# Two edits to a retention-attention and mixture-of-experts kernel: one weight chunk's low part made by GpSimd instead of an accumulating DMA, and a table of powers spread by TensorE instead of loaded whole

## The chip, the cores and the metric

The kernel runs on one core of one Trainium2 chip. The metric is the device time of one execution, in microseconds (us). Engine names are those of the profile: PE is TensorE, ACT is ScalarE, DVE is VectorE, POOL is GpSimd, SP is SyncE, which here only issues DMAs and waits.

## What is computed

The first half is retention attention over 8 batches, 8 heads, 576 positions and head size 64. The second half is a mixture of 8 experts whose input is the attention's output, 4608 tokens of 512 numbers. Each expert takes 576 tokens.

```python
scores = scale * np.matmul(q, k.transpose(0, 1, 3, 2))
gamma = 1.0 - 2.0 ** (-5.0 - np.arange(H, dtype=np.float32))
Dmat = np.where(rel >= 0, gamma[:, None, None] ** rel[None, :, :], 0.0)
attn_out = np.matmul(scores * Dmat, v)
...
logits = x @ w_gate
# tokens go to experts in falling order of their logits, at most N // E = 576 to each
for e in range(E):
    mask = assigned == e
    out[mask] = np.maximum(x[mask] @ w1[e], 0.0) @ w2[e]
```

## The kernel before, in words

**Attention.** `attention` (L498) works through 16 units; a unit u is four batches' worth of one pair of heads, with its own loads of q, k, v and a second layout of k (`qin`, `kin`, `vin`, `nin`). The loads sit in three buffers each, and the load of unit u + 2 is issued when unit u begins. The decay is split in two factors: v is scaled by negative powers (`vscale`, L545, on ACT), and the output by positive powers when it leaves PSUM (`evict`, L621, on DVE, which multiplies by `ex`). `ex` is a [128, 4 x 576] table, the last part of the constants `cst`: for the pair of heads hp, partition p holds 0.125 times the powers 0 to 575 of one head's gamma, one head in partitions 0 to 63 and the other in 64 to 127. Its four pieces of 128 x 576 are loaded by `consts` (L521), two of them among the first loads, the other two when units 1 and 2 begin. `fetch` (L526) issues the first loads on SP in the order of a string; one of them, `q0`, goes out on ACT's queue.

Each half of a unit is a run of small fp32 matmuls: `A` (L557, tile `pA`) makes scores, which DVE masks into `am`; `ST` (L582, tile `pS`) makes the running state, which ACT copies to `S`; `across` and `within` (L594, L604, tile `pX`) make the output. The engines run their instructions in the order in which they are written here (the scheduler is switched off), so an instruction that waits holds up all that stand behind it on its engine. Small pieces of other work are hung on places of the loop with `at(g, ...)`, where g counts nine places to a unit, and `fills` runs them at the end of a half unit.

**Routing and experts.** After the attention, DVE and PE search for the tokens of the first expert (`search_first`, `members`, `listing`), GpSimd gathers their rows with five indirect DMAs (`gather`, L914), and the expert's two matmul layers run. The search for the next expert is threaded through the layers: its counting matmuls (`r`, L332) stand at fixed places among the layer's matmuls, and DVE's small operations (`cs` to `G`) between two counts make the operand of the next.

Weights come in chunks of 128 x 1024: each expert has four of w1 and four of w2, numbered 0 to 7 here. `conv` (L893) takes the next chunk out of `raw` and splits it in a high part `hi` and the rest `lo`, so that three fast matmuls stand in for one in full fp32:

```python
A.activation(hi, raw, AF.Copy)
if fast:
    V.tensor_tensor(lo, raw, hi.bitcast(F32), op=ALU.subtract)
else:
    A.activation(lo, raw, AF.Copy, scale=-1.0)
    nc.gpsimd.dma_start(lo, raw, accum_op=ALU.add)
```

So DVE makes the low part of chunk 0 of the first expert (`conv(True)` in `run`); for all others ACT writes a negated rounded copy and an accumulating DMA, issued by GpSimd, adds `raw` to it. `raw` has four buffers: `dma_pump` (L880) issues the load of a chunk into a buffer once both readers of the chunk that lay there are done.

`l1` (L941) runs the first layer in blocks (f, s): f is one of eight groups of 128 hidden columns, s a part of the tokens (256 or 320 of them); chunk f // 2 holds the weights. A block is 12 matmuls in groups of three, `wh` with `xh`, `wh` with `xl`, `wl` with `xh`; each block ends with ACT's `hb` (L967) and DVE's `hb` (L970). For the first expert the blocks run (0,0), (1,0), (0,1), (1,1), (2,0), (2,1) and on. `conv` is called after the blocks that this line picks (i counts blocks):

```python
if s and f in (1, 2, 4, 6) or e == 0 and i in (0, 2, 4):
    conv()
```

Of the kernel before, what the change touches and what calls it, by code (L numbers as in the profile page):

```python
# [10 lines left out]
F32 = mybir.dt.float32  # L11
# [3 lines left out]
ALU = mybir.AluOpType  # L15
AF = mybir.ActivationFunctionType
AX = mybir.AxisListType

B, H, S, D = 8, 8, 576, 64
NP, HP, NB = 4, 4, 9  # L20
# [5 lines left out]
def consts_np():  # L26
    h = np.arange(H); g = (1.0 - 2.0 ** (-5.0 - h)).astype(np.float64)
    p = np.arange(128)
    at = np.where(np.arange(NB) < 8, 128 * (np.arange(NB) // 2), 512)[None] + np.where(np.arange(NB) < 8, p[:, None], p[:, None] % 64)
    vs = g.reshape(HP, 1, 2)[None] ** -at[:, None, :, None].astype(np.float64)  # L30
    m1 = p[:, None] <= p[None, :]
    m2 = p[:, None] % 64 <= np.arange(64)[None, :]
    ex = 0.125 * g.reshape(HP, 2)[:, p // 64].T[:, :, None] ** np.arange(S)
    f = lambda a: np.ascontiguousarray(a, dtype=np.float32).reshape(128, -1)
    return np.concatenate([f(vs), f(m1), f(m2), f(ex)], axis=1)

# [41 lines left out]
class Route:  # L78
# [9 lines left out]
    def fetch(s, nc, fc_d):  # L88
        s.nc = nc
        s.fc = s.pool.tile([128, fc_d.shape[1]], F32, name="rc_f")  # L90
        nc.sync.dma_start(s.fc, fc_d)
# [405 lines left out]

def attention(tc, nc, P, qk, vk, cst_d, wg_d, rf, xd, Lg):  # L498
    cst = P['c'].tile([128, CST + HP*S], F32, name="cst", tag="xg")
    vs = cst[:, 0:HP*18].rearrange("p (h q) -> p h q", h=HP)  # L500
    m1, m2 = cst[:, CST-192:CST-64], cst[:, CST-64:CST]
    ex = cst[:, CST:].rearrange("p (h q) -> p h q", h=HP)
    wg = P['a'].tile([128, HP, 32], F32, name="wg")
# [16 lines left out]

    def consts(hp):  # L521
        part(CST + S*hp, CST + S*hp + S)
    load(0, "kqvn", (512,))
    load(1, "kqvn", (512,))

    def fetch(order):  # L526
        for x in order.split():
            if x == "c":
                part(0, CST)
            elif x[0] == "h":  # L530
                consts(int(x[1]))
            else:
                (nc.scalar if x == "q0" else nc.sync).dma_start(*pieces[x[0].isupper(), x[0].lower()].pop(0))
    fetch("k0 q0 c v0 n0 k1 q1 h0 v1 n1 K0 Q0 h1 V0 N0 K1 Q1 V1 N1")
    R = Route(P['c'], P['a'], P['ps'], Lg, P['ident'])
# [17 lines left out]
    def A(u, hf):  # L553

        if u == 16: return
        if hf == 0 and 2 <= u + 1 < 16:
            if u < 3:  # L557
                consts(u + 1)
            if u == 2:
                R.fetch(nc, rf)  # L560
                nc.sync.dma_start(wg[:, :, 0:8], wg_d.rearrange("(hp p) e -> p hp e", p=128))
# [191 lines left out]
    A(0, 0)  # L753
    ST(0, 0)
    nc.gpsimd.memset(wg, 0.0)

# [96 lines left out]
def moe(tc, nc, P, R, xd, w1_d, w2_d, out, mix):  # L853
# [38 lines left out]

    def conv(fast=False):  # L893

# [9 lines left out]
        if fast:  # L904
            V.tensor_tensor(lo, raw, hi.bitcast(F32), op=ALU.subtract)
        else:
            A.activation(lo, raw, AF.Copy, scale=-1.0)
            nc.gpsimd.dma_start(lo, raw, accum_op=ALU.add)  # L908
# [32 lines left out]
    def l1(e, tr):  # L941
# [5 lines left out]
        for i, (f, s) in enumerate(order):  # L947
# [24 lines left out]
            mix.vec(340 + 140*s)  # L972
            if s and f in (1, 2, 4, 6) or e == 0 and i in (0, 2, 4):
                conv()
# [61 lines left out]
    def run():  # L1036
# [3 lines left out]
        gather(0)  # L1040
        conv(True)
        mix.step()
        warm(25)
        mix.adv(3500)
# [14 lines left out]

def build(tc, nc, qk, vk, cst, wg, rf, w1, w2, out):  # L1060
    with ExitStack() as top:
        P = {}
# [31 lines left out]
        with ExitStack() as ctx:  # L1094
            Q = dict(P)
            for name, bufs in (("a", 1), ("ld", 2), ("w", 2), ("xt", 2)):
                Q[name] = ctx.enter_context(tc.tile_pool(name="a_" + name, bufs=bufs))
            R, rows = attention(tc, nc, Q, qk, vk, cst, wg, rf, xd, Lg)

# [35 lines left out]
```

## Time and profile before

| | |
|---|---|
| three runs | 650.55, 650.63, 651.21 us; median 650.63 us |
| the profiled execution | 651.56 us |
| its span, first to last instruction | 649.8 us |
| PE busy in the span | 610.9 us (94%) |
| DVE, ACT, POOL busy | 406.5, 288.8, 140.9 us |
| mean granted TensorE clock | 0.986 |
| moved by DMA | 134.20 MB |

The page gives the busy time of each engine and the chain of work that ended last. The timeline rows read: start, duration, engine, line, operation, output <- input, shape, count; in square brackets the idle time of the engine before the row and who ended it. A row with a count over 1 merges instructions that followed each other. Rows marked SPq are DMA issues of the SP queue.

### The profile page before, as it was taken

How to read it: one execution, taken by the hardware profiler on the slowest of the kernel's cores; microseconds unless marked ns; L12 is line 12 of the kernel's file. 1: busy time of each engine (PE TensorE's matmuls, PEld its weight loads, DVE VectorE, ACT ScalarE, POOL GpSimd, SP SyncE). 2: the span in 40 equal slices, each digit the busy share in tenths (PEclk: the TensorE clock that was granted, in tenths of full speed). 3: DMA queues.
4: the chain of work that ended last, by engine and by line, in shares of the span. 5: the costliest groups of instructions: out<-in, count | busy, mean ns of one | idle time of the engine just before them, and what ended most of it. 6: DMA issues, size and time to landing. Idle time of an engine off the chain costs nothing.

```text
span 649.8 us, 14770 instructions
## 1 busy us (share of the span) xinstructions
PE 610.9 (94%) x5756; PEld 519.3 (80%) x5756; DVE 406.5 (63%) x1504; ACT 288.8 (44%) x584; POOL 140.9 (22%) x189
## 2 busy tenths in 40 slices
PE   8899898978969998999999999988999999999995
PEld 5687777756569878977987898788779889989984
DVE  3567979778747887987996897777783302301300
ACT  4455555523265236552563356144615724643500
POOL 0000000000311072162153142241314234131111
PEclk9999999989979999999999999998999999999998
DMA  9998999743497469889599199747966995893521
GB/s 333 400 391 281 348 350 351 266 98 131 155 215 176 140 173 246 212 193 263 110 245 261 59 223 227 208 106 172 201 188 146 227 264 141 174 269 117 98 66 40
DMA packets 51704, 134.20 MB, mean 207 GB/s; under 512 B 5810, under 2 KB 19762, under 8 KB 51634
## 3 DMA queue, kind: packets, MB, share of 16 engines
q0 software_dynamic: 14960, 51.91, 36.7%
q1 hardware_dynamic: 36530, 81.08, 36.0%
q8 instruction: 45, 0.74, 0.5%
q10 hardware_dynamic: 144, 0.26, 0.1%
q14 instruction: 25, 0.20, 0.1%
HBM read 81.33 MB, written 18.87 MB: 154 GB/s over the span
## 4 chain that ended last, share of the span: by engine, by line
PE 68%; DVE 15%; DMA 6%; issue 6%; POOL 2%; ACT 2%; SPq 0%; POOLq 0%; DVEq 0%; ACTq 0%
PE ph L963 25%; PE py L1002 24%; PE pA L566 4%; PE pX L610 3%; DMA qin<-in_qk 2%; PE pS L589 2%; PE pX L601 2%; PE r L332 2%; PE pt L934 2%; DMA w1l<-raw 1%; PE pT L643 1%; DVE am L568 1%; DVE xT L630 1%; POOL xg L919 1%; DMA cst<-in_cst 1%
## 5 line engine op out<-in xcount | busy, mean ns | idle before, releaser
L1002 PE MATMUL py<-w2h,hb 128*128 128x512 f32 x576 | 188.2, 399 | 0.0
L963 PE MATMUL ph<-xh,w1h 128*128 128x320 f32 (+1 forms) x512 | 153.7, 304 | 2.7 <-ACT xh L936 1.5
L963 PE MATMUL ph<-xh,w1l 128*128 128x320 f32 (+1 forms) x512 | 151.3, 299 | 4.6 <-DMA w1l<-raw 4.2
L963 PE MATMUL ph<-xl,w1h 128*128 128x320 f32 (+1 forms) x512 | 151.0, 299 | 0.2 <-issue 0.2
L1002 PE MATMUL py<-w2l,hb 128*128 128x512 f32 (+1 forms) x320 | 125.1, 391 | 0.0
L1002 PEld LDWEIGHTS py<-w2h,hb 128*128 128x128 f32 x576 | 104.0, 188 | 20.6
L963 PEld LDWEIGHTS ph<-xh,w1l 128*128 128x128 f32 x512 | 97.7, 192 | 5.4 <-DMA w1l<-raw 4.4
L967 ACT ACTIVATE hb<-ph 128x256 fp32r<-128x256 f32 (+1 forms) x128 | 51.7, 410 | 112.5 <-PE ph L963 103.9
L963 PEld LDWEIGHTS ph<-xh,w1h 128*128 128x128 f32 x512 | 97.8, 192 | 4.7 <-ACT xh L936 1.9
L963 PEld LDWEIGHTS ph<-xl,w1h 128*128 128x128 f32 x512 | 97.9, 192 | 0.7 <-DVE cs L336 0.3
L970 DVE SCALAR_TENSOR_TENSOR hb<-ph,hb 128x256 fp32r<-128x256 f32 (+1 forms) x192 | 59.0, 352 | 60.2 <-ACT hb L967 56.6
L919 POOL DMA_INDIRECT xg<-xd,idx x40 | 40.8, 1020 | 202.1 <-DMA raw<-in_w 168.8
L1002 PEld LDWEIGHTS py<-w2l,hb 128*128 128x128 f32 (+1 forms) x320 | 56.7, 177 | 12.7
L979 POOL DMA_INDIRECT out_y<-yt,idx x40 | 40.9, 1022 | 118.4 <-ACT yt L1019 76.4
L1019 ACT ACTIVATE yt<-py 128x512 f32<-128x512 f32 x32 | 19.2, 598 | 105.3 <-PE py L1002 79.8
L908 POOL DMA_DIRECT2D w2l<-raw x32 | 28.8, 900 | 126.5 <-ACT hb L967 117.8
L548 ACT ACTIVATE vin<-vin,cst 128x128 f32<-128x128 f32 (+1 forms) x160 | 48.2, 379 | 6.8 <-DMA vin<-in_vk 6.8
L568 DVE TENSOR_TENSOR am<-pA,cst 128x1024 f32<-128x1024 f32 x32 | 39.1, 1221 | 18.0 <-PE pA L566 17.7
L1022 DVE TENSOR_TENSOR yt<-yt,py 64x512 f32<-64x512 f32 x8 | 5.4, 679 | 69.5 <-ACT yt L1021 69.3
L566 PEld LDWEIGHTS pA<-qin,kin 64*128 64x128 f32 x512 | 32.1, 191 | 16.1 <-DVE am L568 7.8
L566 PE MATMUL pA<-qin,kin 64*128 64x128 f32 x512 | 38.3, 289 | 6.9 <-DVE am L568 5.0
L591 ACT ACTIVATE S<-pS 128x128 f32<-128x128 f32 x64 | 17.6, 276 | 51.1 <-PE pS L589 51.1
(177 smaller groups left out, 877.4 us busy)
## 6 DMA issues: line engine op xcount, KB each, us to landing
raw<-in_w SPq DMA_DIRECT2D x64, 512.0 KB, 5.5
w2l<-raw POOLq DMA_DIRECT2D x32, 512.0 KB
w1l<-raw POOLq DMA_DIRECT2D x31, 512.0 KB
kin<-in_qk SPq DMA_DIRECT2D x14, 576.0 KB, 7.2
qin<-in_qk SPq DMA_DIRECT2D x14, 576.0 KB
vin<-in_vk SPq DMA_DIRECT2D x14, 576.0 KB, 7.2
nin<-in_vk SPq DMA_DIRECT2D x14, 512.0 KB, 10.5
xd<-xr SPq DMA_DIRECT2D x36, 192.0 KB, 4.0
```

The lines of the kernel that those rows point to most:

```text
L548: nc.scalar.activation(x, x, AF.Copy, scale=vs[:, u % HP, 4*c+h:4*c+h+1])
L566: nc.tensor.matmul(pa[:, r, j], LD[u, 'k'][half(r), s], LD[u, 'q'][half(r), s], start=True, stop=True, skip_group_check=True)
L568: nc.vector.tensor_tensor(AM[u, hf], pa, m1[:, None, None, :].to_broadcast([128, 2, 4, 128]), op=ALU.mult)
L610: nc.tensor.matmul(PX[u, hf][half(h), b, 128*c:128*c+128], v[:, a:a+64], AM[u, hf][:, h ^ b, j], start=False, stop=False, skip_group_check ...
L908: nc.gpsimd.dma_start(lo, raw, accum_op=ALU.add)
L919: nc.gpsimd.indirect_dma_start(out=xg[:n, j, :], out_offset=None, in_=xd[:, :], in_offset=bass.IndirectOffsetOnAxis(ap=found[e][:n, j:j+1] ...
L963: T.matmul(ps, w, x, start=(k == 0), stop=(k == 11))
L967: A.activation(hb[:, f, c], ps, AF.Relu)
L970: V.scalar_tensor_tensor(hb[:, f, to+a:to+b], ps[:, a:b], 0.0, hb[:, f, 256*s+a:256*s+b].bitcast(F32), op0=ALU.max, op1=ALU.subtract)
L979: st = nc.gpsimd.indirect_dma_start(out=out[:, :], out_offset=bass.IndirectOffsetOnAxis(ap=found[e][:n, t:t+1], axis=0), in_=y[:n], in_off ...
L1002: T.matmul(ps[:m], a, w, start=(k == 0), stop=(k == last), skip_group_check=True)
L1019: A.activation(y, ps, AF.Copy)
```

## The change

Two edits that don't touch each other.

First, the table `ex` is no longer part of the constants in memory. For each pair of heads a [2, 704] array `er` is loaded: two rows, one for each head, with a 0/1 pattern of 128 columns that says which partitions belong to that head, and the head's 576 powers. `spread(hp)` makes the 128 x 576 table of the pair with two fp32 matmuls (contraction over 2 rows, 128 output rows, 288 columns each) and two ACT copies from PSUM. The four loads of `er` stand behind the constants on SP; `spread(0)` runs before the loop, the others at the places 4, 13 and 22.

Second, the split of chunk 1 of the first expert: its `conv` moves from behind block (0,0) to behind the gathers, and its low part is a subtraction on GpSimd.

```diff
-def attention(tc, nc, P, qk, vk, cst_d, wg_d, rf, xd, Lg):
-    cst = P['c'].tile([128, CST + HP*S], F32, name="cst", tag="xg")
+def attention(tc, nc, P, qk, vk, cst_d, er_d, wg_d, rf, xd, Lg):
+    cst = P['a'].tile([128, CST], F32, name="cst")
+    er = [P['c'].tile([2, 128 + S], F32, name="er", tag="raw", bufs=4) for _ in range(HP)]
...
-    ex = cst[:, CST:].rearrange("p (h q) -> p h q", h=HP)
+    ex = P['c'].tile([128, HP, S], F32, name="ex", tag="xg")
...
-    def consts(hp):
-        part(CST + S*hp, CST + S*hp + S)
+    def spread(hp):
+
+        for a in (0, S//2):
+            pe = P['ps'].tile([128, S//2], F32, name="pe", tag="y", bufs=2)
+            nc.tensor.matmul(pe, er[hp][:, :128], er[hp][:, 128+a:128+a+S//2], start=True, stop=True)
+            nc.scalar.activation(ex[:, hp, a:a+S//2], pe, AF.Copy)
...
-            elif x[0] == "h":
-                consts(int(x[1]))
+            elif x == "e":
+                for i in range(HP):
+                    nc.sync.dma_start(er[i], er_d[:, i*(128+S):(i+1)*(128+S)])
...
-    fetch("k0 q0 c v0 n0 k1 q1 h0 v1 n1 K0 Q0 h1 V0 N0 K1 Q1 V1 N1")
+    fetch("k0 q0 c e v0 n0 k1 q1 v1 n1 K0 Q0 V0 N0 K1 Q1 V1 N1")
...
-            if u < 3:
-                consts(u + 1)
...
     ST(0, 0)
+    spread(0)
+    for hp in range(1, HP):
+        at(9*hp - 5, spread, hp)
...
-    def conv(fast=False):
+    def conv(fast=None):
...
         if fast:
-            V.tensor_tensor(lo, raw, hi.bitcast(F32), op=ALU.subtract)
+            fast.tensor_tensor(lo, raw, hi.bitcast(F32), op=ALU.subtract)
...
-            if s and f in (1, 2, 4, 6) or e == 0 and i in (0, 2, 4):
+            if s and f in (1, 2, 4, 6) or e == 0 and i in (2, 4):
                 conv()
...
         gather(0)
-        conv(True)
+        conv(V)
         mix.step()
+        conv(nc.gpsimd)
         warm(25)
```

The order of the first DMAs on SP. Before (`cst` 128x264 is the masks and small constants, `cst` 128x576 a piece of the table):

```order
L533 DMA kin<-in_qk 128x512
L519 DMA cst<-in_cst 128x264
L533 DMA vin<-in_vk 128x512
L533 DMA nin<-in_vk 128x512
L533 DMA kin<-in_qk 128x640
L533 DMA qin<-in_qk 128x640
L519 DMA cst<-in_cst 128x576
L533 DMA vin<-in_vk 128x640
L533 DMA nin<-in_vk 128x512
L533 DMA kin<-in_qk 128x512
L533 DMA qin<-in_qk 128x512
L519 DMA cst<-in_cst 128x576
```

Now:

```order
L544 DMA kin<-in_qk 128x512
L525 DMA cst<-in_cst 128x264
L542 DMA er<-in_er 2x704 x4
L544 DMA vin<-in_vk 128x512
L544 DMA nin<-in_vk 128x512
L544 DMA kin<-in_qk 128x640
L544 DMA qin<-in_qk 128x640
L544 DMA vin<-in_vk 128x640
L544 DMA nin<-in_vk 128x512
L544 DMA kin<-in_qk 128x512
L544 DMA qin<-in_qk 128x512
```

Four small issues have come in ahead of the first `vin`, and the pieces of the table, which stood between the other loads, are gone.

The first matmuls of the attention on PE. Before:

```order
L566 MATMUL pA<-qin,kin 128x128 x8
L589 MATMUL pS<-vin,nin 64x64 x4
L566 MATMUL pA<-qin,kin 128x128 x8
L577 MATMUL pAt<-qin,kin 64x64 x4
L601 MATMUL pX<-qin,S 64x128 x4
```

Now:

```order
L575 MATMUL pA<-qin,kin 128x128 x8
L598 MATMUL pS<-vin,nin 64x64 x4
L531 MATMUL pe<-er 128x288 x2
L575 MATMUL pA<-qin,kin 128x128 x8
L586 MATMUL pAt<-qin,kin 64x64 x4
L610 MATMUL pX<-qin,S 64x128 x4
```

The first spread stands between the first state matmuls and the second group of scores. The other three stand each ahead of a group of scores as well: of the second half of units 1, 2 and 3.

ACT around the first layer of the first expert. Before (`xh` is the high part of the gathered tokens; the first `w1h` is chunk 0, the second chunk 1):

```order
L903 ACTIVATE w1h<-raw 128x1024
L936 ACTIVATE xh<-pt 128x4x128 x2
L967 ACTIVATE hb<-ph 128x256
L903 ACTIVATE w1h<-raw 128x1024
L907 ACTIVATE w1l<-raw 128x1024
L936 ACTIVATE xh<-pt 128x4x128 x2
L936 ACTIVATE xh<-pt 128x4x64
L967 ACTIVATE hb<-ph 128x256
L967 ACTIVATE hb<-ph 128x320
L903 ACTIVATE w1h<-raw 128x1024
L907 ACTIVATE w1l<-raw 128x1024
L967 ACTIVATE hb<-ph 128x320
```

Now:

```order
L915 ACTIVATE w1h<-raw 128x1024 x2
L948 ACTIVATE xh<-pt 128x4x128 x2
L979 ACTIVATE hb<-ph 128x256
L948 ACTIVATE xh<-pt 128x4x128 x2
L948 ACTIVATE xh<-pt 128x4x64
L979 ACTIVATE hb<-ph 128x256
L979 ACTIVATE hb<-ph 128x320
L915 ACTIVATE w1h<-raw 128x1024
L919 ACTIVATE w1l<-raw 128x1024
L979 ACTIVATE hb<-ph 128x320
```

The high part of chunk 1 has moved ahead of all token work and its negated copy is gone; chunk 2 and those after it keep their places. On POOL the first accumulating DMA behind the five gathers has become a `TENSOR_TENSOR` on the same tiles.

## Rows read from the trace of the kernel before

**Rows 1.** The page: the busy share of PE in 40 equal slices of 16.2 us, and the granted TensorE clock in the same slices, in tenths.

```profile
PE   8899898978969998999999999988999999999995
...
PEclk9999999989979999999999999998999999999998
```

**Rows 2.** The longest waits: engine and line, what ended the wait, us in total, times, longest.

```profile
PE ph L963 <- DMA w1l<-raw: 4.2, 1, 4.2
ACT vin L548 <- DMA vin<-in_vk: 6.8, 4, 2.4
```

**Rows 3.** Timeline of the first expert's first layer, ACT: chunk 0's high part, the first `xh`, then block (0,0), chunk 1 and on.

```profile
169.14 1.06 ACT L903 ACTIVATE w1h<-raw 128x1024 fp32r<-128x1024 f32 x1 [1.90 <-DMA raw<-in_w]
174.14 0.60 ACT L936 ACTIVATE xh<-pt 128x512 fp32r<-128x512 f32 x1 [3.94 <-PE pt L934]
...
178.46 1.05 ACT L903 ACTIVATE w1h<-raw 128x1024 fp32r<-128x1024 f32 x1
179.41 1.05 ACT L907 ACTIVATE w1l<-raw 128x1024 fp32r<-128x1024 f32 x1
180.36 1.35 ACT L936 ACTIVATE xh<-pt 128x512 fp32r<-128x512 f32 x3
...
183.82 0.44 ACT L967 ACTIVATE hb<-ph 128x320 fp32r<-128x320 f32 x1 [1.84 <-PE ph L963]
...
198.14 0.37 ACT L967 ACTIVATE hb<-ph 128x256 fp32r<-128x256 f32 x1
```

**Rows 4.** Timeline, PE, the same stretch: the first row is block (0,1), the next the third matmul of block (2,0), the last the third count.

```profile
181.76 0.85 PE L963 MATMUL ph<-xh,w1h 128*128 128x320 f32 x4 [0.80 <-ACT xh L936]
...
189.96 0.58 PE L963 MATMUL ph<-xh,w1l 128*128 128x256 f32 x1 [4.18 <-DMA w1l<-raw]
...
201.96 0.39 PE L332 MATMUL r<-oh,G 128*128 128x32 bf16 x9 [0.23 <-DVE G L163]
```

**Rows 5.** Timeline, POOL: the fifth gather, then the accumulating DMAs of chunks 1 and 2.

```profile
175.56 0.98 POOL L919 DMA_INDIRECT xg<-xd,idx  x1 [0.31 <-issue]
181.06 0.99 POOL L908 DMA_DIRECT2D w1l<-raw  x1 [4.52 <-issue]
186.45 0.89 POOL L908 DMA_DIRECT2D w1l<-raw  x1 [4.39 <-ACT w1l L907]
```

**Rows 6.** Timeline, the SP queue: the loads of chunks 5 and 6, each issued when an accumulating DMA (of chunks 1 and 2) has landed and freed its buffer. Last, the time from issue to landing of all weight loads.

```profile
190.03 0.33 SPq L889 DMA_DIRECT2D raw<-in_w  x1
192.52 0.34 SPq L889 DMA_DIRECT2D raw<-in_w  x1
...
DMA to landing us min/median/max: 3.7/5.5/7.9
```

**Rows 7.** Table by stretches: length, busy time and count of PE, PEld, DVE, ACT and POOL, granted clock, DMA share, GB/s.

```profile
5.00:22.00 17.00, 13.40 (x234) 11.00 (x234) 7.57 (x10) 8.94 (x28) 0.00 (x0) 1.00 1.03 396
30.00:40.00 10.00, 9.91 (x208) 8.76 (x206) 7.71 (x35) 5.63 (x20) 0.00 (x0) 1.00 1.03 406
185.00:190.00 5.00, 0.82 (x7) 0.62 (x5) 1.40 (x6) 3.37 (x5) 1.75 (x2) 0.77 0.94 192
190.00:195.00 5.00, 5.00 (x30) 4.91 (x31) 2.56 (x12) 2.05 (x3) 0.00 (x0) 0.55 1.00 194
195.00:200.00 5.00, 5.00 (x47) 4.90 (x46) 2.55 (x13) 3.38 (x6) 1.71 (x2) 1.00 0.96 279
```

**Rows 8.** The low part of chunk 0, by DVE (min, median, max in ns).

```profile
L905 DVE TENSOR_TENSOR w1l<-raw,w1h x1: 1226/1226/1226, 170.2 to 170.2; 128x1024 fp32r<-128x1024 f32 x1
```

**Rows 9.** The chain that ended last, in its first 22 us.

```profile
0.76 3.99 DMA qin<-in_qk
...
6.58 6.35 DMA cst<-in_cst
...
12.94 8.89 DMA qin<-in_qk
```

**Rows 10.** Timeline of the start: the issue of the first `vin`, the first ACT instruction, and PE up to the first scores of unit 2.

```profile
1.68 0.43 SPq L533 DMA_DIRECT2D vin<-in_vk  x1
...
5.70 1.28 ACT L548 ACT_TABLE_LOAD   x1 [5.70 <-DMA vin<-in_vk]
...
7.44 0.74 PE L589 MATMUL pS<-vin,nin 128*64 128x64 f32 x8 [0.57 <-ACT vin L548]
8.51 1.16 PE L566 MATMUL pA<-qin,kin 64*128 64x128 f32 x16 [0.33 <-DMA qin<-in_qk]
...
11.92 0.45 PE L589 MATMUL pS<-vin,nin 128*64 128x64 f32 x8 [0.39 <-ACT S L591]
...
20.35 0.45 PE L589 MATMUL pS<-vin,nin 128*64 128x64 f32 x8 [0.72 <-ACT S L591]
21.97 1.16 PE L566 MATMUL pA<-qin,kin 64*128 64x128 f32 x16 [1.17 <-DMA qin<-in_qk]
```

**Rows 11.** Prices of PE and ACT work like the spreads': eight matmuls of 128 columns (each two records), twelve transposes of 128 columns (one record each), four matmuls of 384 columns side by side (two records each), and an ACT copy of 384 columns from PSUM.

```profile
14.28 1.05 PE L610 MATMUL pX<-am,vin 128*64 128x128 f32 x16
147.81 1.47 PE L685 MATMUL pT<-ident,xT 128*128 128x128 f32 x12
44.47 0.85 PE L643 MATMUL pT<-xT,wg 128*32 128x384 f32 x8
45.38 0.49 ACT L649 ACTIVATE lt<-pT 128x384 f32<-128x384 f32 x1 [0.46 <-PE pT L643]
```

More of the change, by code (lines that the diff above doesn't have):

```diff
@@ L32, in consts_np, with powers_np @@
     m2 = p[:, None] % 64 <= np.arange(64)[None, :]
-    ex = 0.125 * g.reshape(HP, 2)[:, p // 64].T[:, :, None] ** np.arange(S)
     f = lambda a: np.ascontiguousarray(a, dtype=np.float32).reshape(128, -1)
-    return np.concatenate([f(vs), f(m1), f(m2), f(ex)], axis=1)
+    return np.concatenate([f(vs), f(m1), f(m2)], axis=1)
+def powers_np():
+    h = np.arange(H); g = (1.0 - 2.0 ** (-5.0 - h)).astype(np.float64)
+    e = 0.125 * g.reshape(HP, 2).T[:, :, None] ** np.arange(S)
+    one = np.arange(2)[:, None] == np.arange(128)[None] // 64
+    return np.concatenate([x for i in range(HP) for x in (one, e[:, i])], axis=1).astype(np.float32)
 def layout(q, k, v):
@@ L1058, in moe, with build @@
     return run
-def build(tc, nc, qk, vk, cst, wg, rf, w1, w2, out):
+def build(tc, nc, qk, vk, cst, er, wg, rf, w1, w2, out):
     with ExitStack() as top:
@@ L1097, in build @@
                 Q[name] = ctx.enter_context(tc.tile_pool(name="a_" + name, bufs=bufs))
-            R, rows = attention(tc, nc, Q, qk, vk, cst, wg, rf, xd, Lg)
+            R, rows = attention(tc, nc, Q, qk, vk, cst, er, wg, rf, xd, Lg)
             def idle(what):
@@ L1122 @@
     w2 = np.asarray(moe_w2).reshape(E, 8, 128, DM).transpose(0, 2, 1, 3).reshape(E, 128, 4096)
-    arrays = dict(in_qk=qk, in_vk=vk, in_cst=consts_np(), in_wg=moe_w_gate, in_rf=route_consts(), in_w1=w1, in_w2=w2)
+    arrays = dict(in_qk=qk, in_vk=vk, in_cst=consts_np(), in_er=powers_np(), in_wg=moe_w_gate, in_rf=route_consts(), in_w1=w1, in_w2=w2)
     arrays = {n: np.ascontiguousarray(x) for n, x in arrays.items()}
```

## The prediction

> **What bounds the kernel now.** I read the page first. PE is busy in nearly every slice, so a microsecond counts where PE stands still or runs slowly; the granted clock falls to 0.7 in the slice from 179 to 195 us, the deepest fall of the span [rows 1]. The waits say what happens there: one wait of PE of 4.2 us for the low part of a weight chunk, the longest that a DMA costs it [rows 2]. The timelines of that stretch show why. In the first expert's first layer PE wants the low part of chunk 1 as the third matmul of block (2,0) and gets it at 189.96 [rows 4]. ACT wrote the negated copy at 179.41 [rows 3], GpSimd issued the accumulating DMA at 181.06 [rows 5], and the load that reuses its buffer went out at 190.03 [rows 6], so that DMA took 8.9 us. After the wait PE isn't at its pace: the table by stretches gives a granted clock of 0.55 from 190 to 195, half speed for nearly all of it, and 30 matmuls in those 5 us against 47 in the next 5 at a clock of 1.00; nine in each are small counts [rows 7].
>
> The start is bound by DMA. The chain that ended last runs through loads until 22 us, one of them a piece of the table `ex` [rows 9]; the DMA engines are full from 5 us on [rows 7]; PE waits in four places, the last for the `qin` of unit 2 until 21.97 [rows 10]. ACT's waits for `vin`, 6.8 us in four times, are the first of these loads too [rows 2]. From 30 us on PE is busy 9.91 of 10 us although DMA is as full as before [rows 7]: there PE sets the pace.
>
> **The first expert's layer.** ACT loses one negated copy, POOL one DMA issue, DMA one accumulating transfer; POOL gets one subtraction of 128x1024.
> - *The subtraction.* It can begin when the fifth gather is issued, 175.56 + 0.98 = 176.5 [rows 5]. No row shows such an operation on POOL. Below, it is DVE's time for the same, 1.23 us [rows 8]. Above, the reader sets the bound: up to 8.3 us cost nothing, as PE is there at 184.8 (next item). So the sum holds nothing for it, and its cover is the work of blocks (0,0) to (1,1). The Trainium skill (GPSIMD Engine Reference, Performance versus the Vector engine) advises against this: elementwise work with two inputs is put at 1.96 times DVE's time, an estimate of 2.4 us here; the sum would be the same by it, and no run so far shows it.
> - *Chunk 1's high part.* It stands ahead of the first `xh` on ACT, which was idle from 170.2 to 174.14 [rows 3]. Chunk 0 had landed by 169.14 [rows 3]; chunk 1 is issued next on the same queue, and its 524 KB take 1.3 us at the 396 GB/s of a full DMA [rows 7]. With its copy of 1.05 it is done by about 172. Nothing.
> - *`xh` earlier.* ACT's three later `xh` waited behind chunk 1's two copies until 180.36 [rows 3], and PE waited 0.80 for them in block (0,1) [rows 4]. That goes. PE reaches the third matmul of (2,0) not at 185.6 (where it would have gone on) but at 184.8, and not at 189.96.
> - *Pace.* From there to the third count PE took 201.96 - 189.96 = 12.0 us [rows 4]. About 0.4 is idle at its end. Half speed cost 5.0 x (1 - 21/38) = 2.2 without the counts [rows 7]. Left are 9.4: PE could be at the third count at 194.2.
> - *What is late next.* DVE makes the operand of the third count behind its `hb` of block (3,0), and that waits for ACT's: from ACT's `hb` at 198.14 to the count at 201.96 it is 3.8 us [rows 3, 4]. On ACT the distances are fixed: behind the `hb` of (0,1), now at 183.0, come four pairs of copies (chunks 2 to 5, 1.9 each) and three `hb` (0.3 each), then the `hb` of (3,0) at 191.9. The count can't begin before 195.7. So PE gains **201.96 - 195.7 = 6.3 us**, not 7.8.
> - *Chunk 2.* Its DMA now follows ACT's copy to about 185.65. In the trace it took 192.52 - 186.45 = 6.1 us [rows 5, 6]; that gives 191.7, and PE wants it as the third matmul of (4,0), 6.9 us behind 184.8, at 191.7. It just fits, and the 1.5 us that PE waits at the third count anyway would swallow a small delay. Chunk 5's load on SP no longer waits for an accumulating DMA: it goes out at about 180.4 instead of 190.03 [rows 6], ahead of chunk 2's DMA, and takes the room that chunk 1's leaves.
>
> Behind the third count the order of all engines is as it was, and everything waits for other work, not for a time, so the 6.3 us stay to the end.
>
> **The start.** Gone are four loads of 288 KB, two of them ahead of unit 2. Added are four DMA issues, eight matmuls and eight ACT copies.
> - *Issues.* Each takes SP 0.43 plus a gap, 0.47. Four put the first `vin` from 1.68 to 3.56. In the trace it landed at 5.70 [rows 10], in a queue already full. Now the queue runs dry for a moment. Landing with the same 4.0 us would be 7.6; if only its place among the bytes counted, 5.7. I take 6.4, nearer the lower end: little is issued ahead of it now (660 KB, 1.7 us at 396 GB/s [rows 7]), so it finds the engines nearly free. ACT's first instruction and the first `pS` follow: 8.1 instead of 7.44, done at 8.9.
> - *Spreads.* Eight `pX` matmuls of 128 columns take 1.05 us, two at a time in the halves of the array's columns: 0.26 for one; less the overlap with the next row, 0.22. In proportion 288 columns are 0.5 us. Twelve transposes of 128 columns in 1.47 give 0.12 each, so 0.28; four matmuls of 384 columns side by side in 0.85 give 0.64 at most [rows 11]. I take 0.5 (fp32 with two records for each matmul, as here), so a spread is 1.0 us of PE, between 0.55 and 1.3. The Trainium skill (FP8 and Floating Point Precision) says that true fp32 goes through the array in four passes, an estimate of 0.48 us here; the sum by it would be 0.1 us lower.
> - *ACT.* Eight copies of about 0.42, less than the 0.49 of 384 columns [rows 11], beside an ACT that is busy 8.94 of 17 us [rows 7]. Nothing.
> - *To unit 2.* With `spread(0)` the second scores begin at 9.9 instead of 8.51. From there to 21.97 it was 13.46 us, of which 0.39 + 0.72 + 1.17 were waits for loads and for ACT behind loads [rows 10]. These go, `spread(1)` comes: 11.2 + 1.0, so 22.1. The `qin` of unit 2 is there: two table pieces fewer (590 KB at 396 GB/s, 1.5 us [rows 7]) against the 0.7 of the late `vin`, 21.2. The relief of DMA just pays for the first two spreads: 0.1 later.
> - *After that* PE is the bound, and `spread(2)` and `spread(3)` are 2.0 us with nothing to hide them. Together the start **loses 2.1 us**. With spreads of 0.55 unit 2 begins with its `qin` at 21.2 and 1.1 follow, 0.3 in all; with spreads of 1.3 it is 3.3, and a `vin` at 7.6 would add 1.2. The third and fourth table piece, also gone, free DMA where nothing waits for it.
>
> **Sum.** 2.1 - 6.3 = -4.2 us. The profiled execution takes 651.56 us around a span of 649.8, which would become 647.4; the median of the runs is 0.93 us lower, so 650.63 - 4.2 = **646.4 us**.
>
> **Rivals.**
> - *The wait moves on to chunk 2.* If its DMA takes what chunk 1's took, 8.9 us [rows 5, 6], it lands at 194.5 and PE waits 2.8 us in block (4,0). Such a wait cost clock in the trace; with 2.2 again for that [rows 7] the third count is at 199.2, and of 6.3 us 2.8 are left: 2.8 - 2.1 = 0.7 faster, 649.9 us. For it: the time fits without a margin. Against: chunk 1's DMA shared the engines with three loads, and chunk 2's should find less. 0.17.
> - *The start gains.* If all spreads hide in waits and the first `vin` isn't late, unit 2 begins with its `qin` 1.5 us earlier, and if PE isn't the bound behind it, as the chain through the loads could have it [rows 9], that stays: -1.5 - 6.3, 642.8 us. Against it are the 9.91 of 10 us [rows 7]. 0.12.
> - *Slower: GpSimd is late.* The subtraction is first in POOL's queue behind the gathers and chunk 2's DMA issue stands behind it. If it ends after 188.9, thus takes over 12 us, the gain in the layer is under the 2.1 lost at the start. At 15 us PE goes on 1.7 us later than before: 654.4. For it: nothing of its kind was measured here. Against: ten times DVE's duration. By the same page of the Trainium skill (Architecture) the first call of a freshly loaded routine costs about 6 us more; by that estimate it would end at 185.0 and the sum be 646.6. For being late enough to matter I give 0.04.
> - *The edit doesn't do what it says.* If chunk 1 lands late, ACT's copy holds up the first `xh` and all that follows; each microsecond past 174.14 costs one. It would have to land 4 us behind chunk 0, as far as the fastest and the slowest weight load lie apart [rows 6]; at 6 us behind it would cost 2, 648.4 us. 0.02.
>
> **How the numbers follow.** My forecast has 0.65, with a range of its own of 644.3 to 648.9 (the start's bounds, and 1 us either way in the layer). The range for 8 in 10 takes in the moved wait and most of the gaining start: 643.0 to 650.2. About 0.2%, 1.3 us, is what a measurement here can tell from nothing. Faster by more: the forecast, the gaining start and a small part of the moved wait, 0.80. Within it: most of the moved wait, 0.12. Slower: a late GpSimd, late `xh`, a dearer start with a moved wait, 0.08.
>
> **What would show it.** Right: a `TENSOR_TENSOR` on POOL from about 176.5, done by 184; no wait of PE for `w1l` at (2,0) and a granted clock near 1.00 from 185 to 195; the third count waiting for DVE some 6 us earlier than before, counted from chunk 0's split; the first `vin` landing between 5.7 and 7.6; spreads of about 1.0 us on PE; unit 2's first scores near 22 us, those of its second half 1 us later than before. Wrong: a wait for chunk 2 at (4,0) of over 1.5 us, a second fall of the clock, or unit 3 beginning earlier than before.

## The result: slower, by 3.8 us (2.0 to 5.6)

| | before | after |
|---|---|---|
| median of nine runs | 650.55 us | 652.88 us |
| ratio | | 1.0058 (1.0030 to 1.0086) |
| profiled execution, span | 651.56, 649.8 us | 653.08, 651.3 us |

The forecast was 646.4 us. The 3.8 us are the ratio's, 0.0058 of 650.55; the two medians lie 2.3 us apart. A second comparison of the same kernel (a1_after_again, below) gave 1.0073 (1.0045 to 1.0101).

**The layer.** Lines of the changed kernel are 5 to 13 above those of before. Timeline of the profile after: POOL (last gather, subtraction), then DVE, PE and ACT; the three rows with `r` on PE are the counts.

```profile
178.42 0.98 POOL L931 DMA_INDIRECT xg<-xd,idx  x1 [0.30 <-issue]
179.43 2.38 POOL L917 TENSOR_TENSOR w1l<-raw,w1h 128x1024 fp32r<-128x1024 f32 x1
...
178.65 0.16 DVE L471 TENSOR_TENSOR room<-room,r 128x8 f32<-128x8 f32 x1
178.85 2.99 DVE L472 SCALAR_TENSOR_TENSOR room<-es,room 128x8 f32<-128x8 f32 x1
181.76 1.28 DVE L949 TENSOR_TENSOR xl<-pt,xh 128x512 fp32r<-128x512 f32 x2
...
179.88 0.64 PE L975 MATMUL ph<-xh,w1l 128*128 128x256 f32 x4
183.09 0.74 PE L975 MATMUL ph<-xl,w1h 128*128 128x256 f32 x4 [2.58 <-DVE xl L949]
185.23 1.23 PE L975 MATMUL ph<-xh,w1h 128*128 128x256 f32 x4
...
193.84 0.39 PE L337 MATMUL r<-oh,G 128*128 128x32 bf16 x9
198.16 0.39 PE L337 MATMUL r<-oh,G 128*128 128x32 bf16 x9
203.87 0.39 PE L337 MATMUL r<-oh,G 128*128 128x32 bf16 x9 [1.15 <-DVE G L168]
...
177.16 0.60 ACT L948 ACTIVATE xh<-pt 128x512 fp32r<-128x512 f32 x1 [3.16 <-PE pt L946]
191.20 0.44 ACT L979 ACTIVATE hb<-ph 128x320 fp32r<-128x320 f32 x1 [2.62 <-PE ph L975]
200.03 0.72 ACT L979 ACTIVATE hb<-ph 128x256 fp32r<-128x256 f32 x2
```

The wait for `w1l` is gone [rows 4], as forecast. But DVE's second `room` operation, eight columns wide, takes 2.99 us beside the subtraction; it ends when that ends (181.8). `xl` stands behind it, so PE waits 2.58 us four blocks earlier in the program, and runs at half speed behind that wait as well. The same DVE lines in the profile before:

```profile
175.99 0.17 DVE L467 SCALAR_TENSOR_TENSOR room<-es,room 128x8 f32<-128x8 f32 x1
176.07 1.28 DVE L937 TENSOR_TENSOR xl<-pt,xh 128x512 fp32r<-128x512 f32 x2
```

There the narrow operation took 0.17 us, although the fifth gather ran on POOL from 175.56 to 176.54 [rows 5]: the gather doesn't hold it. Table by stretches, after:

```profile
10.00:16.00 6.00, 5.45 (x61) 4.93 (x62) 1.42 (x2) 2.26 (x8) 0.00 (x0) 0.50 1.03 393
...
185.00:190.00 5.00, 5.00 (x23) 4.93 (x23) 4.09 (x18) 1.08 (x3) 0.00 (x0) 0.50 0.85 333
190.00:195.00 5.00, 5.00 (x43) 4.96 (x42) 1.56 (x8) 3.80 (x6) 1.00 (x1) 0.92 0.01 2
```

One standstill of PE is gone and another has come, with the same fall of the clock to 0.50 behind it. From the first `xh` to the third count it was 27.8 us [rows 3, 4] and is 26.7: of the 6.3 us that were forecast the layer gained 1.1.

**The start.** Timeline after: the SP queue, ACT, PE.

```profile
1.71 1.21 SPq L542 DMA_DIRECT2D er<-in_er  x4
2.96 0.36 SPq L544 DMA_DIRECT2D vin<-in_vk  x1
5.05 0.43 SPq L544 DMA_DIRECT2D qin<-in_qk  x1
...
6.13 1.28 ACT L559 ACT_TABLE_LOAD   x1 [6.13 <-DMA vin<-in_vk]
...
8.14 0.47 PE L598 MATMUL pS<-vin,nin 128*64 128x64 f32 x8 [1.51 <-ACT vin L559]
8.55 1.23 PE L531 MATMUL pe<-er 2*128 2x288 f32 x4
10.55 2.08 PE L575 MATMUL pA<-qin,kin 64*128 64x128 f32 x16 [0.77 <-DMA qin<-in_qk]
16.36 1.31 PE L575 MATMUL pA<-qin,kin 64*128 64x128 f32 x16
24.42 1.16 PE L575 MATMUL pA<-qin,kin 64*128 64x128 f32 x16
29.15 1.16 PE L575 MATMUL pA<-qin,kin 64*128 64x128 f32 x16
```

Standstills of 1.51 and 0.77 us frame the first spread, and from 10 to 16 us the clock is at 0.50 (the first row of the table above); before it was 1.00 there. Unit 2 begins at 24.42 instead of 21.97 [rows 10], and everything up to the first `xh` is 3.0 us later (177.16 against 174.14 [rows 3]). In this pair of profiles 3.0 us are lost here, 1.1 won in the layer and 0.4 behind the third count: the span grows by 1.5 us.

### The profile page after: what moved, and what is told of

The parts are those of the page before. It is cut to its first block, busy times and chain, and to the rows that moved or that the text cites. A ratio compares the mean times of both kernels' runs of the same rounds, so it can differ in the third digit from the quotient of the medians.

```text
span 651.3 us, 14808 instructions
## 1 busy us (share of the span) xinstructions
PE 615.5 (95%) x5768; PEld 523.2 (80%) x5772; DVE 409.4 (63%) x1504; ACT 290.7 (45%) x591; POOL 142.2 (22%) x189
## 3 DMA queue, kind: packets, MB, share of 16 engines
q0 software_dynamic: 14816, 51.39, 35.5%
## 4 chain that ended last, share of the span: by engine, by line
PE 64%; DVE 15%; issue 10%; DMA 6%; ACT 2%; POOL 1%; SPq 0%; POOLq 0%; ACTq 0%; DVEq 0%
PE py L1014 24%; PE ph L975 20%; PE pA L575 4%; PE pX L619 4%; DMA raw<-in_w 2%; PE pS L598 2%; PE pX L610 2%; PE pt L946 2%; PE r L337 2%; DMA qin<-in_qk 1%; PE pT L652 1%; DVE am L577 1%; DVE G L168 1%; DVE xT L639 1%; DMA w2l<-raw 1%
## 5 line engine op out<-in xcount | busy, mean ns | idle before, releaser
L920 POOL DMA_DIRECT2D w2l<-raw x32 | 28.8, 900 | 119.8 <-ACT hb L979 109.6
L575 PEld LDWEIGHTS pA<-qin,kin 64*128 64x128 f32 x512 | 32.9, 196 | 16.2 <-DVE am L577 7.1
```

Of the source, the lines that this page charges most:

```text
L575: nc.tensor.matmul(pa[:, r, j], LD[u, 'k'][half(r), s], LD[u, 'q'][half(r), s], start=True, stop=True, skip_group_check=True)
```

## The experiments

Each run was compared with the kernel before on the same chip. There were five such comparisons, each on its own chip, where the median of before was between 645.0 and 648.2 us: e1 to e4; b1, a1, s1 and s2; e3_again, s3, s5 and s2_again; e6 to e8 and s1_again; s1_beside_s3 and s3_beside_s1. Absolute times are set side by side within one of them only. One execution of each run was profiled. "Listing" is the start of the listing's matmuls (`r<-rh`, at the end of the attention), "layer" the time from there to the third count, "half" the time at half speed in the first 20 us by the granted clock in tables of 2 us stretches.

| run | against before, us | ratio (95%) | listing | layer | half |
|---|---|---|---|---|---|
| before, first profile | | | 166.5 | 35.5 | 0 |
| b1_before_again | (one run) | | 163.0 | 34.6 | 0 |
| after, first profile | +2.3 | 1.0058 (1.0030-1.0086) | 169.5 | 34.4 | 6.8 |
| a1_after_again | +4.2 | 1.0073 (1.0045-1.0101) | 169.1 | 34.1 | 6.8 |
| e1_split_alone | -3.5 | 0.9947 (0.9921-0.9973) | 164.7 | 34.5 | 3.4 |
| e2_start_alone | +4.0 | 1.0067 (1.0040-1.0094) | 167.9 | 37.3 | 3.4 |
| e3_no_collision | -5.6 | 0.9910 (0.9884-0.9937) | 164.6 | 30.4 | 6.8 |
| e3_again | -5.3 | 0.9916 (0.9885-0.9947) | 164.8 | 29.1 | 3.4 |
| e4_fill_wait | -4.3 | 0.9937 (0.9914-0.9959) | 164.2 | 31.5 | 0 |
| e6_both_on_dve | -3.5 | 0.9941 (0.9921-0.9962) | 164.0 | 30.4 | 0 |
| s1_both_no_collision | -0.2 | 0.9999 (0.9971-1.0028) | 168.8 | 30.6 | 6.8 |
| s1_again | -0.2 | 0.9994 (0.9973-1.0016) | 168.8 | 29.9 | 6.8 |
| s1_beside_s3 | -1.0 | 0.9982 (0.9962-1.0002) | 167.1 | 31.0 | 6.8 |
| s3_filled_start | -3.6 | 0.9955 (0.9933-0.9978) | 164.2 | 30.1 | 0 |
| s3_beside_s1 | -4.2 | 0.9944 (0.9918-0.9969) | 165.6 | 29.0 | 0 |
| s5_rows_no_spread | -2.7 | 0.9952 (0.9929-0.9975) | 167.4 | 30.4 | 6.8 |
| s2_rows_later | -1.1 | 0.9992 (0.9963-1.0021) | 163.9 | 31.8 | 0 |
| s2_again | -0.7 | 0.9981 (0.9951-1.0011) | 168.3 | 29.6 | 10.2 |
| e7_old_start_filled | -3.9 | 0.9955 (0.9936-0.9975) | 163.8 | 28.8 | 0 |
| e8_two_fills | -4.8 | 0.9941 (0.9918-0.9964) | 165.8 | 29.2 | 0 |

A single profile places the marks of the start only within some 3 us: the same program (s2) had its listing at 163.9 and at 168.3 us, with 0 and 10.2 us at half speed ahead of it. So the start is judged by the comparisons, the profiles tell what happens. A 0 under "half" isn't always full speed either: in e4 and e6 the clock reads 1.00, but the second scores took 2.08 us, as they do at 0.50, where others took 1.16.

### Each edit alone, and both again

e1 is the kernel before with the diff's lines on `conv` alone, e2 the kernel after without them; b1 and a1 are the two kernels unchanged.

> The kernel before with the GpSimd edit alone, the table loaded as before. Collision theory: DVE's second room operation (0.17 us before) again takes about 3 us beside GpSimd's subtraction of 2.4 us, PE waits some 2.6 us for xl in block (0,0), runs at half speed behind it, and the third count comes about 1 us earlier than before, at 200.9; the time is 649.5 us against 650.6. Rival, that the loss is all in the start and this edit gives what was forecast: third count at 195.7, 644.3 us.

> The changed start alone, chunk 1 split as before. From the trace of the change: all marks from the last attention unit on 3.0 us later, so 653.6 us, with the granted clock at half from about 10.5 to 16 us. The forecast had 2.1 us (652.7). Rival, that the two edits need each other (the start is free without the other): 650.6.

> The kernel before, nothing edited, for a profile on the chip of the other runs of this set. The split alone gained 3.5 us in its comparison while its layer was only 1.0 us shorter than that of the first trace, from the listing's matmuls to the third count (34.5 against 35.5 us). If the wait for chunk 1's low part varies between executions (4.2 us in the first trace, 6.2 in that of the changed start alone), this profile has a wait over 5 us and a stretch near 37; the rival, that the layer before is always as in the first trace, has 35.5 and then the gain came from elsewhere.

> The kernel after, nothing edited, compared again. If the two edits simply add, 0.9947 x 1.0067 = 1.0014 of before, and 1.0058 was at the far end of its scatter; if they work against each other, 1.0058 again. In the profile the collision is there in both cases: the room operation near 3 us, PE's wait near 2.6.

The signs separate: the split gains, the start loses. e1 shows the collision again, with the old start (DVE, then POOL):

```profile
174.17 2.98 DVE L467 SCALAR_TENSOR_TENSOR room<-es,room 128x8 f32<-128x8 f32 x1
...
174.74 2.37 POOL L905 TENSOR_TENSOR w1l<-raw,w1h 128x1024 fp32r<-128x1024 f32 x1
```

e1 gained more than the 1.1 us expected. The layer of before isn't always the same: its wait for `w1l` was 4.18, 3.07 (b1) and 6.18 us (e2), the layer 34.6 to 37.3, against 34.1 to 34.5 in the three profiles with the collision. b1's wait, expected over 5, was the shortest of them. By these profiles the gain is anything from 0.1 to 2.8 us; e1's interval, 1.7 to 5.1 us, overlaps that. Nor do the edits add up: -3.5 and +4.0 give 0.6 us slower for both, and a1 measured 4.2. This is taken up below.

### The collision taken away

`room` is updated by two operations: a sum with the counts, which reads one operand from PSUM, and one with both operands in SBUF, the one that took 2.99 us. e3 is e1 with the second moved ahead of the rest of DVE's work there, so that only the sum stays in its place:

```diff
-    def room(s, cn):
+    def room(s, cn, early=False):
         V = s.nc.vector
-        V.tensor_tensor(s.nr, s.nr, cn, op=ALU.add)
+        if not early:
+            V.tensor_tensor(s.nr, s.nr, cn, op=ALU.add)
         V.scalar_tensor_tensor(s.nr, s.es, -1.0e6, s.nr, op0=ALU.mult, op1=ALU.min)
...
             s.taken()
+            s.room(None, early=True)
...
-            s.room(cn)
+            s.nc.vector.tensor_tensor(s.nr, s.nr, cn, op=ALU.add)
```

> As e1, but the room operation with two operands in SBUF runs ahead of the search's other DVE work, before the gathers end; what is left beside the subtraction reads one operand from SBUF and one from PSUM. Collision theory: that operation takes 0.2 us, xl starts at about 176.1 as before, PE waits for nothing there, its clock stays at 1.00, and the third count comes at 195.7 as forecast: 650.6 - 6.3 = 644.3 us. Rival, that GpSimd's subtraction holds any DVE work or DVE waited for something else: xl ends with the subtraction again, third count and time as in e1 (649.5).

> The third experiment's kernel again (old start, split without the collision), as the common base of the three that follow. 0.991 of before again (0.988 to 0.994), listing's matmuls near 164.6 us.

Timeline of e3: DVE, POOL (first gather, subtraction), PE (first and third count).

```profile
170.31 0.16 DVE L468 SCALAR_TENSOR_TENSOR room<-es,room 128x8 f32<-128x8 f32 x1
173.68 0.16 DVE L497 TENSOR_TENSOR room<-room,r 128x8 f32<-128x8 f32 x1
...
175.52 0.69 DVE L939 TENSOR_TENSOR xl<-pt,xh 128x512 fp32r<-128x512 f32 x1 [0.82 <-ACT xh L938]
177.70 0.42 DVE L972 SCALAR_TENSOR_TENSOR hb<-ph,hb 128x256 fp32r<-128x256 f32 x1 [1.49 <-ACT hb L969]
...
168.17 2.16 POOL L921 DMA_INDIRECT xg<-xd,idx  x1 [166.92 <-ACT w1h L905]
175.69 2.41 POOL L907 TENSOR_TENSOR w1l<-raw,w1h 128x1024 fp32r<-128x1024 f32 x1
...
184.44 0.39 PE L332 MATMUL r<-oh,G 128*128 128x32 bf16 x9
194.93 0.39 PE L332 MATMUL r<-oh,G 128*128 128x32 bf16 x9 [1.60 <-DVE G L163]
```

`xl` and `hb` run at their usual lengths in the middle of the subtraction; both have one operand in PSUM. GpSimd's work alone doesn't hold DVE. The moved operation takes 0.16 us, long before the subtraction. In this execution, however, GpSimd was late: the first gather took 2.16 us instead of 1.13 (after), and the subtraction began 2.0 us behind the sum on `room`. In the profile after it was 0.78 us. e3_again has that distance again, DVE and POOL:

```profile
174.08 0.16 DVE L497 TENSOR_TENSOR room<-room,r 128x8 f32<-128x8 f32 x1
174.16 1.28 DVE L940 TENSOR_TENSOR xl<-pt,xh 128x512 fp32r<-128x512 f32 x2
...
174.86 2.40 POOL L908 TENSOR_TENSOR w1l<-raw,w1h 128x1024 fp32r<-128x1024 f32 x1
```

With everything in the place that it has in the profile after, less the one operation, `xl` runs on into the subtraction at its usual length. The wait is gone in both profiles, the clock stays at 1.00 from 180 to 195, and the layer takes 30.4 and 29.1 us where 29.2 was forecast (195.7 less the listing at 166.47). The theory of the collision stands, its rival falls. In the comparisons taking the collision away gave 2.2 us with the old start (e1 to e3) and 4.4 with the changed one (a1 to s1).

The Trainium skill states the rule (SBUF — State Buffer, section "Who interferes with whom"): a DVE instruction with two inputs in SBUF contends with a GpSimd instruction that reads SBUF, for ports that only one of them can hold; outside DVE's two-port modes, one with at most one such input doesn't contend. Both halves agree with these rows: 2.99 us against 0.17 for the operation on `room`, the usual 0.69 and 0.42 us for `xl` and `hb`. The page also lets the order of issue decide which of the two waits. The rows don't show that: the DVE operation is recorded 0.58 us ahead of the subtraction, and it was held.

The collision is a race, and not every execution need lose it. All four profiles with the collision (after, a1, e1, e4) have 0.77 or 0.78 us from the sum to the subtraction. In five of the 20 profiles (e3, e6, s2, s3, s5) the first gather took 1.98 to 2.19 us; where the subtraction followed on GpSimd it began 1.6 to 2.0 us behind the sum, and an operation of 0.17 us would have been over in time. Of e1's eleven executions four took 639.1 to 640.8 us, like e3's (638.0 to 640.4), at a mean clock of 0.994 to 0.998; the other seven took 642.3 to 645.2, at 0.984 to 0.992, the profiled one among them. By that clock the two at 0.997 and 0.998 were at half speed for some 4 us at most in all (an estimate: 0.003 of 638 us are lost, and half speed loses half of its stretch), where the profiled one was for 6.8 us behind the collision alone. None of the four was profiled, so that they had no collision is likely, not shown.

e4 leaves the collision in, but gives PE work in the wait:

```diff
             for k, (w, x) in enumerate(terms):
+                if e == 0 and i == 0 and k == 8:
+                    warm(10)
```

> As e1, with ten dummy matmuls of 512 columns (0.233 us each, 2.3 in all) on PE just ahead of the three matmul groups that wait for xl, so that PE doesn't stand still there. Theory, that the fall of the clock follows from PE's standstill: granted clock near 1.00 behind the wait, 5.8 us of half speed go, third count some 2.9 us earlier than in e1 (198.0), 646.6 us. Rival, that the clock falls at this place whatever PE does: third count and time as in e1 or 0.2 later (649.7).

```profile
177.82 0.74 PE L965 MATMUL ph<-xl,w1h 128*128 128x256 f32 x4 [0.29 <-DVE xl L937]
...
195.73 0.39 PE L332 MATMUL r<-oh,G 128*128 128x32 bf16 x9 [1.15 <-DVE G L163]
```

No half speed follows, and the layer is 31.5 us against e1's 34.5: 3.0 us, as expected (2.9). So more than half of what the collision cost in e1's profile (4.1 to 5.4 us, against e3's two) was clock. What went is the 6.8 us at half speed of e1, not the 5.8 expected. In the comparison e4 is only 0.9 us under e1, but all its executions (640.4 to 642.2 us) are under e1's seven long ones.

e6 is e1 with the subtraction on DVE:

```diff
-        conv(nc.gpsimd)
+        conv(V)
```

> e1 with chunk 1's low part made by DVE instead of GpSimd, at the same place in the program. The subtraction takes DVE 1.23 us ahead of its search work, so xl comes 1.2 us later than in the kernel before instead of 2.9 with the collision; PE waits about 1 us. If a wait of 1 us doesn't cost the clock: third count 33 us or less behind the listing's matmuls, 0.990 to 0.993. If it does: 33 to 34, 0.994 like e1.

```profile
170.57 1.22 DVE L905 TENSOR_TENSOR w1l<-raw,w1h 128x1024 fp32r<-128x1024 f32 x1
174.22 0.17 DVE L467 SCALAR_TENSOR_TENSOR room<-es,room 128x8 f32<-128x8 f32 x1
...
175.81 0.64 PE L963 MATMUL ph<-xl,w1h 128*128 128x256 f32 x4
```

The expected wait of 1 us did not come: PE takes up `xl` at 175.81 without one. In this execution the late first gather (1.98 us) made PE wait 0.88 us for the rows ahead of that, which hid DVE's extra work; where the gather is early it may not be hidden. The layer is as short as e3's, 30.4 us. In time e6 gained 3.5 us, on another chip than e3; on its own chip it was 0.4 us over e7 (below), which keeps the subtraction on GpSimd without the collision and fills a wait at the start. So no gain of GpSimd over DVE is shown here.

### The start

s1 is the kernel after with e3's edit. s3 fills PE's standstill in it:

```diff
     A(0, 0)
+    P['warm'](6)
     ST(0, 0)
```

s2 is s1 with the loads of `er` issued later and `spread(0)` behind the second scores:

```diff
-    fetch("k0 q0 c e v0 n0 k1 q1 v1 n1 K0 Q0 V0 N0 K1 Q1 V1 N1")
+    fetch("k0 q0 c v0 n0 k1 q1 e v1 n1 K0 Q0 V0 N0 K1 Q1 V1 N1")
...
             if hf == 0:
                 A2(u)
+            if u == 0 and hf == 0:
+                spread(0)
```

s5 is e3 with four idle loads of `er`'s size in `er`'s place and no spreads:

```diff
+            elif x == "e":
+                for i in range(HP):
+                    nc.sync.dma_start(er[i], cst_d[0:2, 128*i:128*i + 128 + S])
...
-    fetch("k0 q0 c v0 n0 k1 q1 h0 ...
+    fetch("k0 q0 c e v0 n0 k1 q1 h0 ...
```

e7 is e3 with `P['warm'](5)` at s3's place, e8 the same with `P['warm'](7)` ahead of the last unit's second `across`.

> Both edits, with the room operation moved ahead as in the third experiment. If the start's loss is by itself (4.3 us) and the collision was the layer's whole fault, 0.9910 x 1.0067 = 0.9976 of before, about 1.5 us faster than before, and some 3 us faster than both edits with the collision. If the late start were made up for by a layer without waits, 0.991.

> s1 again (both edits, no collision, start as changed), in one comparison with a filled old start. Half clock from about 9 to 16 us and listing's matmuls near 168.8 again; 0.997 to 1.000 of before, some 0.4% over the filled one (0.9955 in its comparison).

> s1 (both edits, no collision, start as changed) beside its filled twin. 0.9997 of before as in two comparisons; about 6.8 us at half speed from 8 to 16 us, listing's matmuls near 168.8.

> Both edits without the collision (s1), with six dummy matmuls of 512 columns on PE between the first scores and the first state matmuls, where PE stood still 1.5 to 1.9 us. If the half clock from 10 to 16 us is what the standstill costs and half speed is the larger part of the start's loss: granted clock near 1.00 there, A(1,0) at 14 us instead of 16, listing's matmuls 1.5 to 2.5 us earlier than in s1 (166.5 to 167.5). Rival, the loss is spreads and late loads: clock restored, but the time unchanged (168.8), since the loads of unit 1 come no earlier.

> s3 (s1 with six dummy matmuls in PE's standstill) beside s1. If the half clock is the loss: 2 to 4 us under s1 in this comparison too, listing's matmuls near 164.3. If the earlier difference was between the chips: within 1 us of s1.

> The old start (table by its own loads, no spreads) on the split without collision, with four small loads of the size of er put where the change has them, into tiles that nothing reads. It takes the issues alone. If the late issue of vin and qin is a large part of the start's loss: second scores near 10.5 us, half clock behind, listing's matmuls 1.5 to 2.5 us later than in the base (166 to 167). Rival, the spreads are the loss (4 x 1.2 us) and unit 2 waits for its qin anyhow: listing as in the base, 164.6.

> As s1, with the four loads of er issued behind the second kin and qin, and the first spread behind the second scores. Theory, that the start's loss beyond the spreads is the late issue of qin and the half clock behind PE's standstill: second scores at 8.5 to 9 us instead of 10.5, no half clock for long, A(2,0) 1 to 2 us earlier, 1 to 2 us faster than s1 (0.995 to 0.996 of before). Rival, that the loss is the four spreads of 1.2 us alone: same as s1.

> s2 again (er issued later, the first spread behind the second scores), beside its base. It takes the spreads alone. In its first profile the listing's matmuls came at 163.9 us, as early as with the old start, but its time was only 0.9 us under s1's. If the profile was typical and the spreads are paid for by the loads that go: listing at 163.5 to 165, time within 1.5 us of the base's. If the spreads cost their 4.8 us less some 2 us of waits: listing near 167, time 3 us over the base's.

> e3 (old start, split without collision) with five dummy matmuls of 512 columns between the first scores and the first state matmuls. Theory: the old start loses clock there in some executions only (three of six profiles, 3.3 to 6.8 us at half speed), so the fill gives less than in the new start: 0.5 to 2 us, 0.988 to 0.991 of before. Rival, the fill is worth its 4.6 us (the new start's) here too: 0.985; or nothing: 0.9916.

> e7 with seven more dummy matmuls where PE waits 1.7 us for xT in the last attention unit, behind which the clock was at half for 3.4 us in most profiles. Up to 1.7 us faster than e7 where PE is the bound behind it, 0 where DVE is: 0.986 to 0.990, listing's matmuls at 161 to 164 us.

s1 and s3 in one comparison, PE (s1 first) and the stretch from 10 to 18 us of each:

```profile
7.83 0.74 PE L600 MATMUL pS<-vin,nin 128*64 128x64 f32 x8 [0.99 <-ACT vin L561]
10.85 2.08 PE L577 MATMUL pA<-qin,kin 64*128 64x128 f32 x16 [1.12 <-DMA qin<-in_qk]
16.66 1.27 PE L577 MATMUL pA<-qin,kin 64*128 64x128 f32 x16
24.68 1.16 PE L577 MATMUL pA<-qin,kin 64*128 64x128 f32 x16
...
10.00:18.00 8.00, 7.15 (x84) 6.39 (x88) 2.13 (x4) 3.42 (x13) 0.00 (x0) 0.57 1.02 390
```

```profile
6.58 1.47 PE L1100 MATMUL warm<-full 128*128 128x512 bf16 x6
10.28 1.16 PE L577 MATMUL pA<-qin,kin 64*128 64x128 f32 x16 [0.40 <-DMA qin<-in_qk]
13.46 1.16 PE L577 MATMUL pA<-qin,kin 64*128 64x128 f32 x16
21.37 1.16 PE L577 MATMUL pA<-qin,kin 64*128 64x128 f32 x16
...
10.00:18.00 8.00, 7.72 (x148) 6.65 (x148) 4.10 (x6) 4.54 (x16) 0.00 (x0) 1.00 1.03 381
```

With the standstill filled the second scores come hardly earlier, but nothing behind them runs at half speed; unit 2 begins 3.3 us earlier, and the median is 3.2 us lower (641.29 against 644.52). Beside e3_again, s3 is 1.7 us slower (641.40 against 639.67), which the two intervals just tell apart: that is left for the spreads. s5, which has the four issues and no spread, is 2.6 us slower than e3_again, with 6.8 us at half speed. So the start's loss is two things: the late loads with the slow clock behind them, 2.6 to 3.2 us (the 3.2 hold some of the second fall told below), and the spreads, about 1.7. That is 4.3 to 4.9 us; s1 lies 4.3 to 5.4 us above e3 when each is set against before.

s2 was to remove the first and didn't, reliably: one of its profiles has no half speed, the other 10.2 us of it, and s2_again was 4.7 us slower than e3_again, where 1.5 or 3 had been expected. PE stands still between the first scores and the scaled `vin` in the old start as well (e1, e3, e3_again: 1.26 to 1.49 us, then 3.4 to 6.8 us at half speed); the change makes it longer and the fall the rule. Filling it in the old start (e7, e8) gave nothing that the comparisons show: 0.9955 and 0.9941 beside e3's 0.9910 and 0.9916, on another chip.

Without the collision the two edits nearly add: e3's -5.6 and -5.3 with e2's +4.0 give -1.6 and -1.3 us, and s1 measured -0.2, -0.2 and -1.0. With it they don't: a1 has +4.2 where 0.6 was expected. Part of this may be the race: a1 has no short executions (651.0 to 655.1 us, clock 0.981 to 0.989), and without e1's four the median of e1 would be 643.9 us, 2.0 under before instead of 3.5. The rest stays open. So does the second fall of the clock in s1: in its three profiles the third count waits 2.2 to 2.4 us (1.4 to 1.6 in e3 and s3) and the clock is at half once more behind it, between 196 and 204 us; at 188 to 189 us ACT had waited 0.6 to 1.5 us for a weight load, which it does there in neither e3 nor s3. What makes this load late with the changed start was not tried.

The version to keep is e3: 5.6 and 5.3 us faster than before in two comparisons.

## Why the prediction was wrong, step by step

- *"So the sum holds nothing for it"* is the step that failed. The subtraction's start and length were right (behind the gathers, 2.38 us, where the prediction's estimate by the Trainium skill was 2.4; the 6 us more of a first call did not show), and so was the time at which its reader needs it. But its cover was judged by the reader alone. What DVE does in those 2.4 us was not looked at: an operation on `room`, with `xl` behind it and PE behind `xl`. In the rows of before it stands at 175.99, half a microsecond ahead of the forecast start of the subtraction; at its 0.17 us it would have been over 0.4 us ahead of it, so even beside these rows it would have looked like a near miss. In the pair of profiles it cost 5.2 of the 6.3 us; in the comparisons, where not every execution need have it, 2.2 and 4.4.
- *Chunk 1's high part, `xh`, pace, the limit by ACT*: right once the collision is away. From `hb` of (0,1) to the third count the forecast had 12.7 us; after it was 12.67 (191.20 to 203.87). Without the collision the layer takes 28.8 to 31.8 us, forecast 29.2; e3 gains 5.3 to 5.6 us in time, forecast 6.3.
- *Chunk 2 just fits*: right. It cost no wait in the profile after, and 0.36 and 0.60 us in two others.
- *The start loses 2.1* is the second step that failed: the direction was right, the term too small; it measured 4.0 (2.6 to 6.1) in e2. The first `vin` (issue 2.96, landing 6.13, states at 8.14) came as forecast (3.56, 6.4, 8.1). Two things were missed. The four issues also delay what stands behind `vin`: the second `qin` went out at 5.05 instead of 3.10, and the second scores waited for it until 10.55, not 9.9. And the longer standstill cost the clock, for which the start had no term, though [rows 7] showed this price in the layer. A spread was 1.16 us instead of 1.0. Of reading only, without weight in the sum: [rows 10] has five waits of PE, not four.
- *The relief of DMA pays for the first two spreads*: half right. The waits for `qin` are gone, and with the clock held all four spreads leave 1.7 us, not 2.1.
- *Rivals.* Faster had 0.80 and slower 0.08, so the side was wrong. The mechanism that was named for slower was wrong too: GpSimd was not late. Chunk 2 did not take the wait over, and the start did not gain. The wait moved to a place that no rival named.

## What to carry to other kernels

Work that moves to GpSimd is to be laid beside DVE's rows of the same microseconds, with a margin, and not only beside its reader: here a DVE operation of 128x8 with both operands in SBUF was held for 2.99 us, until GpSimd's subtraction ended. It could be moved out of the way, and operations with an operand in PSUM were not held. Waits of PE like these can cost twice, themselves and half speed behind them: those of 2.58 to 6.18 us in the layer did in every profile, those of 1.0 to 1.9 us at the start did in most. It isn't sure: s2's third count waited 2.40 us and the clock stayed at 1.00. A change that only moves such a wait gains little, and a few dummy matmuls in it (e4, s3) gave back what the clock took.

## What was not expected of the hardware

- DVE's blocked operation is recorded from 178.85, GpSimd's subtraction only from 179.43, and the first still waited for the second's end. By the records the later one won; in e1 the same (174.17 and 174.74).
- Four small loads of two rows went out in 1.21 us on SP, 0.30 each, where large ones took 0.43 [rows 10].
- The granted clock reads 1.00 in the first microseconds of a profile while the first scores take 2.08 us, nearly twice their 1.16 and as long as at 0.50 (10.55 in the profile after): there the length of the matmuls tells the speed, not the column.
- The same accumulating DMA of one chunk made PE wait 3.07, 4.18 and 6.18 us in three profiles with that code (b1, before, e2).
